# One planned order for attention, router and experts: whole groups of value products, direct router logits, two weight parts staged early

## The chip, the cores and the metric

The kernel runs on one NeuronCore of a Trainium2 chip. The metric is the device time in microseconds (us). The engines are named as the profile names them: PE (TensorE matmul), PEld (its weight loads), DVE (VectorE), ACT (ScalarE), POOL (GpSimd) and SP (SyncE, which here only issues DMAs).

## The reference

Three layers on 4 x 576 tokens. Attention has 8 heads of 64, and keeps in each row only the scores within tau of the row's maximum. A mixture of 8 experts follows, in which each token goes to one expert (512 to 1024 to 512, with relu); a router weighs it. A dense layer ends it (512 to 2048 to 512, leaky relu). All is float32.

```
scores = scale * np.matmul(q, k.transpose(0, 1, 3, 2))
thresh = np.max(scores, axis=-1, keepdims=True) - tau
scores = np.where(scores >= thresh, scores, -1000000000.0)
...
logits = x @ w_gate;  e_idx = np.argmax(logits, axis=1)
eom = 1.0 / (1.0 + np.exp(-(x @ w_output_gate)))
h = np.maximum(x[mask] @ w1[e], 0.0);  ye = h @ w2[e]
out[mask] = gate_w[mask, None] * eom[mask, e, None] * ye
...
h = x @ w_in;  g = np.maximum(0.01 * h, h);  g @ w_out
```

## The kernel before

Work is not issued in program order. Each step (a handful of instructions) is added to a `Plan` with an engine or a choice of two, a cost in us, what it depends on, a priority and the buffers it takes and frees. `Plan.run` places the steps one after another: on each engine it looks when each ready step could start, keeps those within TOL = 0.0499 us of the earliest, and takes among them the one of lowest priority number. The order so found is fixed at build time; on the chip every engine runs its own instructions in that order and waits on semaphores. A step that is late on the chip thus holds up all that stands behind it on its engine. There are two plans: one for attention (with the router and the first expert products at its end) and one for all that follows.

**Attention** handles two heads at a time: 16 pairs, each with 9 tiles of 128 queries. For a tile PE makes the scores (label S, L447, products in float32r, 4 instructions of 288 columns), DVE takes the row maximum (L456), ACT the exponential (L467), DVE masks and sums (L475), PE transposes the result (TR, L504, 4 transposes in float32), and ACT or DVE copies it out of PSUM. The products with the values (AV, L583) need all tiles of a half pair: each half has four chunks of 4 instructions on 64 columns of the array (two heads side by side), and a last chunk on all columns (L589). The plan places the chunks one by one, so that other PE work can come between two of them. Eight PSUM banks are shared: a score tile holds two of them, every transpose and every half of AV one.

**Router logits** per pair: G0 (L641) multiplies with the gate matrix as the stationary operand, 32 columns of the array for each of four token groups; ACT copies the result out (L232, tile g); X1 transposes it back (L654), adds one direct product for the fifth token group (L655, the tokens as the stationary operand, 32 columns streamed) and transposes the fifth group (L656). After the last pair of a batch a chain of small DVE steps ranks tokens.

**First tokens.** `prefix`, at the end of the attention plan, picks the expert with most tokens after three batches, loads the four parts of its first-layer weights into `raw`, and runs the first layer for 216 of its tokens (L1439) on PE while the last batch is being ranked.

**Experts** (second plan). Weights come as 512 KB parts (L1571) through 4 `raw` buffers; each part is cast (hi, L1538) and its remainder taken (lo, L1543), and three products (hi hi, hi lo, lo hi) stand for one in float32. The first tokens' second layer comes first (L1683, parts 4 to 7), then eight windows of tokens, one for each expert, of 400 down to 216 tokens (L1642 first layer, L1683 second). Tokens are gathered by POOL, transposed by PE and cast by ACT and DVE. A branch on a flag (L1991, all engines) stands where the plan reaches t_over = 2.2. Besides, `narrow` (L1289 to L1326) turns the dense layer's weights, whose 8-byte elements are read as pairs of integers, into float32: two staging buffers `dw`, four DVE steps and one ACT step (L1317) for each of 32 blocks. It starts at plan time w_n0 = 30. The dense layer (L1845, L1871) ends the kernel.

Of the kernel before, what the change touches and what calls it, by code (L numbers as in the profile page):

```python
# [61 lines left out]
class Plan:  # L62
# [8 lines left out]
    START, DONE = 1.1, 0.9  # L71

    def __init__(self):
        self.ops = []
        self.dma = 0.0
        self.hook = None
# [16 lines left out]
    def run(self):  # L93
# [11 lines left out]
        for o in self.ops:  # L105
            if o.left == 0:
                enter(o)
        done = []
        while len(done) < len(self.ops):
# [29 lines left out]
            o.eng, o.t0, o.t1 = e, s, s + o.engs[e]  # L139
            engs[e] = o.t1  # L140
            if o.dma:
# [49 lines left out]
def attention(ctx, tc, q, k, v, st):  # L191
# [61 lines left out]
    for P in range(NP):  # L253
# [49 lines left out]
        def turn(o, P=P):  # L303
            T["sw", P] = t = one.tile([128, 9, 2, D], F32R, name="sw")
            nc.scalar.copy(out=t[:, :, 1, :], in_=T["srk", P][:, :, 0, :].bitcast(F32))
            nc.vector.tensor_copy(out=t[:, :, 0, :], in_=T["srk", P][:, :, 1, :].bitcast(F32))
# [49 lines left out]
        for h in range(2):  # L356
            a = pl.add(
                "pe", 0.22, lambda o, P=P, h=h: trs(o, T["srk", P], range(4 * h, 4 * h + 4)), [O["lrk", P], O.get(("k1", P))],
                base + st.w_k[h], acq=[(bk, 1), (r_tp, 1)] + ([(r_k1, 1)] if h == 0 else []), label="trk",
# [8 lines left out]
        a = pl.add(  # L368
            "pe", 0.11, tail_tr, [O["lrk", P], O["lrq", P], O["k1", P]], base + st.w_k[2], acq=[(bk, 1), (r_tp, 1)], label="trt",
        )  # L370
# [9 lines left out]
        for h in range(2):  # L380
            a = pl.add(
                "pe", 0.22, lambda o, P=P, h=h: trs(o, T["srq", P], range(4 * h, 4 * h + 4)), [O["lrq", P], O.get(("qt", P)), *used],
                base + st.w_k[3 + h], acq=[(bk, 1), (r_tp, 1)] + ([(r_qt, 1)] if h == 0 else []),
# [18 lines left out]
        else:  # L402
# [18 lines left out]
            for h in range(3):  # L421
                a = pl.add("pe", 0.22, lambda o, h=h, f=trs2: f(o, h), [sw], -8.2 + h, acq=[(bk, 1), (r_tp, 1)], label="trk2")
# [7 lines left out]
        for i in range(9):  # L430
# [41 lines left out]
            def mask(o, P=P, n=n, h=h, t=t, rP=rP):  # L472
# [11 lines left out]
            s = O["s", n] = pl.add(  # L484
                "pe", 0.98 if i == 8 else 0.49, scores, [O["k2", P], *kev, *qev, O.get(("s", n - 1))], n + st.w_s,
                acq=[(bk, 2), (r_sc, 1)],
# [89 lines left out]
        for half in range(2):  # L576
# [18 lines left out]
            for c in range(5):  # L595
                box = {}
                prev = pl.add(
                    "pe", 0.53 if c < 4 else 0.49,
                    lambda o, f=av, c=c, fb=first: f(o, fb or o, c), [*ready[half], prev, O.get(("av", P))],
                    base + st.w_av + (5 * half + c) * st.d_av, acq=[(bk, 1), (r_av, 1)] if c == 0 else [],  # L600
                    rel=[(r_et, O["t", base]), (r_rv, O["rv", P])] if (half, c) == (1, 4) else [], label="AV",
                )
# [35 lines left out]

        def g0(o, xP=xP, hp=hp):
            for t in range(4):  # L640
                nc.tensor.matmul(  # L641
                    out=bank(o)[32 * t:32 * t + 32, 0:128], lhsT=gd[:, hp, :], rhs=xP[:, t * 128:(t + 1) * 128],
                    start=True, stop=True, tile_position=(0, 32 * t),
                )

        def g0_ev(o, a, P=P):
            T["g", P] = sm_p.tile([128, 128], F32, tag="g", name="g", bufs=2)
            copy(o, T["g", P], bank(a)[:, 0:128])

        ag = O["xo1", P] = pl.add("pe", 0.29, g0, [*xr, gates], wx + 0.1, acq=[(bk, 1), (r_tp, 1)], label="G0")  # L650
        eg = pl.add(AD, evac(128), lambda o, a=ag, f=g0_ev: f(o, a), [ag], wx + 0.5, rel=[(bk, ag), (r_tp, ag)], label="eG0")

        def x1(o, P=P, xP=xP, hp=hp):
# [22 lines left out]

        a1 = O["xo2", P] = pl.add("pe", 0.43, x1, [*xr, eg], wx + 1, acq=[(bk, 1), (r_tp, 1)], label="X1")
        e2 = pl.add("dve", 0.24, lambda o, a=a1, f=x2_ev: f(o, a), [a1, rc], wx + 1.5, label="eX2")
# [712 lines left out]

def prefix(pl, tc, st, R, w1, xrows, done):

# [119 lines left out]
def experts(pl, ctx, tc, st, R, ar, w1, w2, w_in, w_out, xrows, yT, wtab, wf, out):  # L1513
# [44 lines left out]
    for r, n, tw in wins:  # L1558
# [7 lines left out]
        for q in range(4 if r is None else 0, 8):  # L1566
# [9 lines left out]
            def lo(o, ld, h):  # L1576
                t = ar.w(h.slots[r_w][0])
                subtract(o, t[:, 1, :], raw[ld.slots[r_raw][0]], t[:, 0, :].bitcast(F32))

            ld = O["ld", r, q] = prev_ld = pl.add(  # L1580
                "sp", 0.4, load, [rl], need - 24, after=[prev_ld], acq=[(r_raw, 1)], dma=1.6 if r is not None else 0.0,
                lat=0.0 if r is not None else (0.0, 0.0, 2.0, 4.0)[q - 4], label="ld")
            a = O["hi", r, q] = prev_hi = pl.add(
                AD, (1.05, 0.8), lambda o, f=hi, ld=ld: f(o, ld), [ld, prev_hi], need - 12, acq=[(r_w, 1)], label="hi", at=0.0 if r is None else free)
            O["lo", r, q] = pl.add(
                *((("dve", "pool"), (1.5, 2.7)) if r is not None else ("dve", 1.4)), lambda o, f=lo, ld=ld, h=a: f(o, ld, h), [a], need - 11.9, rel=[(r_raw, ld)], label="lo", at=free)
# [325 lines left out]
def tile_attn_moe_mlp(ctx, tc, q, k, v, tau, w_gate, w_ogate, w1, w2, w_in, w_out, out):  # L1912
# [8 lines left out]
    st.nsc, st.ntp, st.nav = 4, 4, 2  # L1921
    st.w_k = [-9.01, -41.3, -10.8, -7.75, -2.8]
    st.w_s, st.w_m, st.w_th, st.w_x, st.w_kk, st.w_t, st.w_te = -0.83, -9.42, -28.19, 3.88, -7.61, 2.26, -14.75
    st.w_l = [-0.74, 7.52]
    st.w_av, st.d_av = 17.36, -0.34
    st.w_xo = 17.33
    st.w_rt, st.w_ch = 11.17, 12.27
    st.w_n0, st.w_n1 = 30, 30
    st.t_over = 2.2
# [5 lines left out]
    st.raw = [raw_p.tile([128, 1024], F32, name=f"raw{i}") for i in range(4)]  # L1935
    st.sm = [raw_p.tile([128, DM], F32, name=f"sm{i}") for i in range(4)]

    xrows = dram.tile([NT, DM], F32, name="xrows")
# [4 lines left out]
    with ExitStack() as order:  # L1943
# [28 lines left out]
        R.wt = rtt  # L1972
        st.prefix = lambda pl, done: prefix(pl, tc, st, R, w1, xrows, done)
        st.batch_done, st.count, st.consts = R.batch, R.count, R.consts
# [6 lines left out]
        with ExitStack() as c2:  # L1981
            p = c2.enter_context(tc.tile_pool(name="ex", bufs=1))
            ar = Arena(p)
            st.ys = [p.tile([128, CAPS[0]], F32, name=f"ys{i}") for i in range(2)]
            st.dw = [p.tile([128, 512, 2], I32, name=f"dw{i}") for i in range(2)]
            st.cv = [p.tile([128, 512], I32, name=f"cv{i}") for i in range(2)]
# [52 lines left out]
```

## Time and profile before

| | us |
|---|---|
| median of 3 runs (1016.75, 1020.75, 1367.39) | 1020.75 |
| profiled execution | 1020.31 |
| its span, first to last instruction | 1018.5 |
| PE busy | 978.2 (96%) |
| DVE busy | 648.4 (64%) |
| ACT busy | 512.5 (50%) |
| POOL busy | 253.2 (25%) |
| mean granted TensorE clock | 0.983 |

Shares are of the whole span. Attention takes its first third, and DVE and ACT are far busier there than the mean shows. A busy PE is not one at its peak: a matmul record covers its time in the pipeline, and what one costs is read from start to start.

### The profile page before, as it was taken

Reading aid. Unit: us, or ns where it says so; the run is one execution under the profiler, and the core shown is the slowest. Engines: PE = TensorE matmul, PEld = TensorE weight load, DVE = VectorE, ACT = ScalarE, POOL = GpSimd, SP = SyncE. Lnnn points to the kernel's source line nnn. Section 1 sums busy time; section 2 is a strip of 40 time slices with the busy share of each in tenths; the row PEclk is TensorE's granted clock in tenths of the full one; section 3 lists DMA queues with packets and bytes.
Section 4 is the critical chain, followed back from the end, with each engine's and each line's share of the span. In section 5 each row is a group of like instructions: output and inputs, shape, how many; then the busy total and the mean of one; then the engine's idle time right before and its main releaser. Section 6 shows DMA issues by size and latency. Waiting matters only on the chain. (4 is left out here: it accounts for less than half of the span.)

```text
span 1018.5 us, 16995 instructions
## 1 busy us (share of the span) xinstructions
PE 978.2 (96%) x6134; PEld 834.6 (82%) x6134; DVE 648.4 (64%) x1255; ACT 512.5 (50%) x1022; POOL 253.2 (25%) x304
## 2 busy tenths in 40 slices
PE   6999999999999799799899999999999999999994
PEld 6777777777787698799899998888888888888883
DVE  6888998998896677997876657994223222322331
ACT  6787787787785253544555535443222322322321
POOL 3433243234121244353424501331000100100000
PEclk9999999999999899799999999999999999999998
DMA  5432432432213588888886753421100200100000
GB/s 145 128 86 60 141 76 71 120 81 64 84 26 104 182 271 257 288 276 271 282 271 209 231 169 93 121 86 42 42 1 1 83 1 0 57 6 1 11 32 21
DMA packets 63580, 114.33 MB, mean 112 GB/s; under 512 B 15424, under 2 KB 32832, under 8 KB 62976
## 3 DMA queue, kind: packets, MB, share of 16 engines
q1 hardware_dynamic: 56912, 92.02, 28.3%
q0 software_dynamic: 6576, 21.15, 7.5%
q8 instruction: 50, 0.82, 0.3%
q14 instruction: 42, 0.34, 0.1%
HBM read 84.72 MB, written 19.09 MB: 102 GB/s over the span
## 5 line engine op out<-in xcount | busy, mean ns | idle before, releaser
L1845 PE MATMUL ps<-arena 128*128 128x512 f32 (+1 forms) x960 | 207.6, 368 | 0.0
L1871 PE MATMUL ps<-arena 128*128 128x512 f32 x864 | 206.7, 389 | 0.0
L1543 DVE TENSOR_TENSOR arena<-raw,arena 128x512 fp32r<-128x512 f32 (+2 forms) x135 | 133.1, 990 | 112.2 <-PE ps L1871 67.1
L1845 PEld LDWEIGHTS ps<-arena 128*128 128x128 f32 x960 | 168.7, 188 | 30.8
L1538 ACT CAST arena<-raw 128x1024 fp32r<-128x1024 f32 (+2 forms) x155 | 123.2, 806 | 131.9 <-PE ps L1871 57.9
L1871 PEld LDWEIGHTS ps<-arena 128*128 128x128 f32 x864 | 161.4, 188 | 33.0
L1856 DVE TENSOR_TENSOR raw<-ps,raw 128x512 f32<-128x512 f32 (+1 forms) x80 | 50.6, 636 | 135.4 <-ACT raw L1852 135.2
L1683 PE MATMUL ps<-arena 128*128 128x216 f32 (+7 forms) x864 | 129.0, 308 | 2.5 <-DVE arena L1656 1.3
L1642 PE MATMUL ps<-arena 128*128 128x400 f32 (+7 forms) x768 | 116.3, 312 | 11.1 <-ACT arena L1538 6.2
L1683 PEld LDWEIGHTS ps<-arena 128*128 128x128 f32 x864 | 123.0, 194 | 3.4 <-DVE arena L1656 1.6
L1642 PEld LDWEIGHTS ps<-arena 128*128 128x128 f32 x768 | 113.1, 194 | 12.6 <-ACT arena L1538 6.7
L456 DVE TENSOR_REDUCE nm<-ps 128x1 f32<-128x576 f32 x144 | 108.7, 755 | 20.5 <-PE ps L447 17.6
L1852 ACT ACTIVATE raw<-ps 128x512 f32<-128x512 f32 (+1 forms) x80 | 44.1, 555 | 152.4 <-PE ps L1845 152.4
L475 DVE SCALAR_TENSOR_TENSOR em<-ps,th,e 128x576 f32<-128x576 f32 x144 | 115.9, 805 | 1.9 <-ACT e L467 1.4
L467 ACT ACTIVATE e<-ps,nm 128x576 f32<-128x576 f32 x144 | 106.7, 742 | 2.5 <-DVE nm L456 2.5
L447 PE MATMUL ps<-k,qt 128*128 128x288 f32 x512 | 104.6, 329 | 1.3 <-DVE em L475 1.0
L447 PEld LDWEIGHTS ps<-k,qt 128*128 128x128 f32 x512 | 75.8, 194 | 31.6 <-DVE em L475 8.2
L232 ACT COPY eta<-ps 128x512 f32<-128x512 f32 (+1 forms) x157 | 83.5, 544 | 25.2 <-PE ps L504 25.0
L1900 POOL DMA_INDIRECT out_dram<-sm,oidx x18 | 17.7, 982 | 304.3 <-ACT sm L1894 271.4
L504 PE MATMUL ps<-ident,em 128*128 128x128 f32 x576 | 85.4, 276 | 0.8 <-DVE em L475 0.8
L583 PE MATMUL ps<-eta,rv 128*64 128x288 f32 x512 | 83.8, 425 | 0.6 <-ACT k L232 0.5
L504 PEld LDWEIGHTS ps<-ident,em 128*128 128x128 f32 x576 | 68.1, 141 | 4.9 <-ACT e L467 2.6
(226 smaller groups left out, 1041.8 us busy)
## 6 DMA issues: line engine op xcount, KB each, us to landing
raw<-in_moe_w_dram SPq DMA_DIRECT2D x72, 512.0 KB, 5.5
k<-k POOLq DMA_DIRECT2D x30, 304.0 KB, 4.1
dw<-in_moe_w_in_dram SPq DMA_DIRECT2D x16, 512.0 KB, 5.3
dw<-in_moe_w_out_dram SPq DMA_DIRECT2D x16, 512.0 KB, 5.2
rk<-in_k_dram SPq DMA_DIRECT2D x16, 256.0 KB, 2.9
rq<-in_q_dram SPq DMA_DIRECT2D x16, 256.0 KB, 3.0
rv<-in_v_dram SPq DMA_DIRECT2D x16, 256.0 KB, 2.7
xrows<-xt SPq DMA_DIRECT2D x4, 1024.0 KB, 4.8
```

Of the source, the lines that this page charges most:

```text
L447: nc.tensor.matmul(out=s[:, c, :], lhsT=lhs, rhs=T[kk, P][:, off + c * HALF:off + (c + 1) * HALF], start=(m == 0), stop=(m == 2 * len(ops) ...
L456: nc.vector.tensor_reduce(out=T["nm", n], in_=T["sc", n], axis=AX.XY, op=ALU.max, negate=True)
L467: nc.scalar.activation(out=T["e", n].rearrange("p (a c) -> p a c", a=2), in_=T["sc", n], func=AF.Exp, bias=T["nm", n][:, 0:1], scale=1.0,)
L475: nc.vector.scalar_tensor_tensor(out=T["em", P, t][:, h, :].rearrange("p (a c) -> p a c", a=2), in0=T["sc", n], scalar=T["th", n][:, 0:1], ...
L504: nc.tensor.transpose(out=bank(o)[:, c * 128:(c + 1) * 128], in_=T["em", P, t][:, h, 64 * h + c * 128:64 * h + (c + 1) * 128], identity=ident,
L583: nc.tensor.matmul(out=out[64 * h:64 * h + 64], lhsT=T["rv", P][:, 4 * h + c, :], rhs=T["eta", P][:, h, c, lo_:lo_ + HALF], start=(c == 0) ...
L1538: nc.scalar.copy(out=out, in_=in_)
L1543: (nc.vector if o.eng == "dve" else nc.gpsimd).tensor_tensor(out=out, in0=in0, in1=in1, op=ALU.subtract)
L1642: nc.tensor.matmul(out=bank(o)[:, 0:n], lhsT=w[:, wi, 128 * f:128 * f + 128], rhs=xx[:, xi, c, :], start=(c == 0 and i == 0), stop=(c == K ...
L1683: nc.tensor.matmul(out=bank(first, d)[:, 0:n], lhsT=w[:, wi, k0:k0 + 128], rhs=hx[:, xi, :], start=(f == 0 and i == 0), stop=(f == 7 and i ...
L1845: nc.tensor.matmul(out=bank(o)[:, 0:n], lhsT=w[:, wi, c, 128 * c2:128 * c2 + 128], rhs=y[:, c, 0:n], start=(k == 0), stop=(k == 3 * KD - 1),)
L1871: nc.tensor.matmul(out=bank(first, t), lhsT=g[:, gi, 128 * t:128 * t + 128], rhs=w[:, wi, c2, :], start=(f == 0 and k == 0), stop=(f == FF ...
```

## The change

Five edits, in one kernel. First, `Plan` gets a price for PE's turn from one kind of step to another: 0.095 from or to AV, -0.08 from float32 to float32r. It is added to the start of a candidate, so that a step of another kind counts as 0.095 later than the next chunk of AV, which is more than TOL. Some PE costs are set anew, and so are the priorities of attention (st.w_...). Second, G0, its copy and the transpose back go; X1 makes the logits of all five token groups as direct products. Third, parts 4 and 5 of the first tokens' second layer are loaded in attention by SP, behind the first-layer parts, into the `dw` buffers, which now exist from the start (`sw` shares the buffers of k2 for that). Their cast and remainder get the lowest plan times, ahead of the branch; the casts of parts 6 and 7 are bound to ACT, and lose their stated load latency of 2 and 4. Fourth, `narrow` starts at 60 and not 30, and its due times end 60 before the dense layer and not 30. Fifth, two small table steps of DVE (`others`, `starts`) come 7 and 14 later.

```
+    def turn(self, a, b):
+        if a is None or not self.KIND:
+            return 0.0
+        a, b = self.KIND.get(a.label, "f"), self.KIND.get(b.label, "f")
+        if a == b:
+            return 0.0
+        if "v" in (a, b):
+            return 0.095
+        return -0.08 if b == "r" else 0.0
...
-                    s = max(t, o.est)
+                    s = max(t + (self.turn(ahead, o) if e == "pe" else 0.0), o.est)
...
+    pl.KIND = {"S": "r", "trk": "r", "trt": "r", "trq": "r", "trk2": "r", "AV": "v"}
...
-                "pe", 0.98 if i == 8 else 0.49, scores, [O["k2", P], ...
+                "pe", 1.064 if i == 8 else 0.532, scores, [O["k2", P], ...
...
-                    "pe", 0.53 if c < 4 else 0.49,
+                    "pe", 0.48 if c < 4 else 0.42,
...
-        ag = O["xo1", P] = pl.add("pe", 0.29, g0, [*xr, gates], wx + 0.1, ...
-        eg = pl.add(AD, evac(128), lambda o, a=ag, f=g0_ev: f(o, a), [ag], ...
         def x1(o, P=P, xP=xP, hp=hp):
-            nc.tensor.transpose(out=bank(o)[:, 0:128], in_=T["g", P], identity=ident)
-            nc.tensor.matmul(out=bank(o)[:, 128:160], lhsT=xP[:, 512:640], rhs=gd[:, hp, :], start=True, stop=True)
+            for t in range(5):
+                nc.tensor.matmul(
+                    out=bank(o)[:, 32 * t:32 * t + 32], lhsT=xP[:, 128 * t:128 * t + 128], rhs=gd[:, hp, :], start=True, stop=True)
             nc.tensor.transpose(out=bank(o)[:, 160:288], in_=xP[:, 512:640], identity=ident)
...
+    for q in range(4, 6):
+        def second(o, q=q):
+            nc.sync.dma_start(out=wview(staged(st, q), q), in_=wpart(w1, w2, st.star, q))
+        last = pl.add("sp", 0.4, second, [last], pr + 1, lat=5.0, label="ld")
...
+            if r is None and q < 6:
+                t = staged(st, q)
+                a = prev_hi = O["hi", r, q] = pl.add("act", 0.3, ... -40 + q, acq=[(r_w, 1)], label="hi")
+                O["lo", r, q] = pl.add("dve", 0.7, ... [a], -40 + q, label="lo")
+                continue
...
-                lat=0.0 if r is not None else (0.0, 0.0, 2.0, 4.0)[q - 4], label="ld")
+                lat=0.0, label="ld", at=free if (r, q) == (0, 1) else 0.0)
-                AD, (1.05, 0.8), lambda o, f=hi, ld=ld: f(o, ld), ...
+                *((AD, (1.05, 0.8)) if r is not None else ("act", 0.2)), lambda ...
...
-    others = pl.add("dve", 1.2, R.others, [], -13, at=free, label="tb")
-    starts = pl.add("dve", 1.3, R.starts, [], 5, at=free, label="tb")
+    others = pl.add("dve", 1.2, R.others, [], -13, at=free + 7, label="tb")
+    starts = pl.add("dve", 1.3, R.starts, [], 5, at=free + 14, label="tb")
...
-    st.w_rt, st.w_ch = 11.17, 12.27
-    st.w_n0, st.w_n1 = 30, 30
+    st.w_rt, st.w_ch = 24.07, -0.65
+    st.w_n0, st.w_n1 = 60, 60
```

## Rows read from the trace of the kernel before

**Rows 1.** Busy us by stretch: PE, PEld, DVE, ACT, POOL; clock, DMA share, GB/s.
```profile
63.40:83.20 19.80, 19.80 (x154) 14.94 (x152) 16.46 (x38) 15.42 (x36) 6.49 (x11) 1.00 0.31 77
103.00:122.70 19.70, 19.70 (x153) 14.84 (x152) 18.30 (x45) 15.08 (x35) 6.12 (x11) 1.00 0.49 144
sum 294.90, PE 294.19 PEld 224.40 DVE 258.59 ACT 231.97 POOL 97.20; mean PE 19.61 PEld 14.96 DVE 17.24 ACT 15.46 POOL 6.48
```
**Rows 2.** PE in order of time, attention: start us, us, engine, line, operation, count.
```profile
27.18 1.01 PE L583 MATMUL ps<-eta,rv 128*64 128x288 f32 x4
...
156.90 0.60 PE L504 MATMUL ps<-ident,em 128*128 128x128 f32 x4
157.43 0.71 PE L583 MATMUL ps<-eta,rv 128*64 128x288 f32 x4
158.07 0.79 PE L447 MATMUL ps<-k,qt 128*128 128x288 f32 x4
...
306.53 0.60 PE L504 MATMUL ps<-ident,em 128*128 128x128 f32 x4
306.88 0.78 PE L447 MATMUL ps<-k,qt 128*128 128x288 f32 x4
...
328.63 2.16 PE L583 MATMUL ps<-eta,rv 128*64 128x288 f32 x16
330.72 0.75 PE L589 MATMUL ps<-etl,vt 128*128 128x288 f32 x2
```
**Rows 3.** The two largest groups of DVE in attention, on the page.
```profile
L456 DVE TENSOR_REDUCE nm<-ps 128x1 f32<-128x576 f32 x144 | 108.7, 755 | 20.5 <-PE ps L447 17.6
L475 DVE SCALAR_TENSOR_TENSOR em<-ps,th,e 128x576 f32<-128x576 f32 x144 | 115.9, 805 | 1.9 <-ACT e L467 1.4
```
**Rows 4.** PE in order of time, the router's products of two pairs.
```profile
306.13 0.27 PE L654 MATMUL ps<-ident,g 128*128 128x128 f32 x1
306.25 0.31 PE L655 MATMUL ps<-gd,xu 128*128 128x32 f32 x2
306.39 0.31 PE L656 MATMUL ps<-ident,xu 128*128 128x128 f32 x1
...
322.02 0.60 PE L624 MATMUL ps<-ident,xu 128*128 128x128 f32 x4
...
322.91 0.59 PE L1419 MATMUL ps<-ident,sm 108*128 108x108 f32 x4
```
**Rows 5.** All engines in order of time, between attention and the experts.
```profile
340.11 6.07 PE L1439 MATMUL ps<-sm,raw 128*128 128x216 f32 x32
...
343.78 0.16 DVE L1089 TENSOR_SCALAR flag<-mcap 128x1 int32<-128x1 f32 x1
344.17 1.99 ACT L1538 CAST arena<-raw 128x1024 fp32r<-128x1024 f32 x2 [11.08 <-DVE flag L1089]
...
349.75 0.57 DVE L1076 TENSOR_TENSOR scr<-one,tsa 128x224 f32<-128x224 f32 x1 [5.81 <-DVEq L1992]
...
351.64 0.67 DVE L1656 SCALAR_TENSOR_TENSOR arena<-ps,arena 128x216 fp32r<-128x216 f32 x2 [0.68 <-SPq L1992]
...
353.50 2.47 PE L1683 MATMUL ps<-arena 128*128 128x216 f32 x10 [0.88 <-DVE arena L1543]
```
**Rows 6.** Busy us by stretch, as in the first group, early in the experts.
```profile
350.00:360.00 10.00, 7.59 (x33) 7.07 (x34) 8.52 (x17) 5.79 (x13) 3.99 (x4) 0.50 0.60 202
...
400.00:410.00 10.00, 5.03 (x29) 4.62 (x28) 9.54 (x11) 5.47 (x8) 4.53 (x4) 0.89 0.93 316
410.00:420.00 10.00, 7.33 (x28) 6.94 (x29) 9.07 (x11) 4.81 (x10) 5.89 (x3) 0.60 1.00 383
```
**Rows 7.** ACT and PE in order of time, at PE's waits in the experts.
```profile
406.56 0.67 ACT L1317 ACTIVATE dw<-dw 128x512 f32<-128x512 f32 x1 [4.17 <-DVE cv L1305]
...
410.73 0.68 PE L1642 MATMUL ps<-arena 128*128 128x368 f32 x1 [5.70 <-ACT arena L1538]
...
488.12 8.84 PE L1642 MATMUL ps<-arena 128*128 128x320 f32 x48 [2.56 <-DVE arena L1656]
```

More of the change, by code (lines that the diff above doesn't have):

```diff
@@ L108, in run @@
         done = []
+        ahead = None
         while len(done) < len(self.ops):
@@ L139, in run @@
             o.eng, o.t0, o.t1 = e, s, s + o.engs[e]
+            if e == "pe":
+                ahead = o
             engs[e] = o.t1
@@ L303, in turn @@
         def turn(o, P=P):
-            T["sw", P] = t = one.tile([128, 9, 2, D], F32R, name="sw")
+            T["sw", P] = t = k1_p.tile([128, 1216], F32R, tag="k2", name="sw")[:, 0:1152].rearrange("p (t a d) -> p t a d", t=9, a=2)
             nc.scalar.copy(out=t[:, :, 1, :], in_=T["srk", P][:, :, 0, :].bitcast(F32))
@@ L484, in attention @@
             s = O["s", n] = pl.add(
-                "pe", 0.98 if i == 8 else 0.49, scores, [O["k2", P], *kev, *qev, O.get(("s", n - 1))], n + st.w_s,
+                "pe", 1.064 if i == 8 else 0.532, scores, [O["k2", P], *kev, *qev, O.get(("s", n - 1))], n + st.w_s,
                 acq=[(bk, 2), (r_sc, 1)],
@@ L636, in attention, with x1 @@
         e0 = pl.add("dve", 0.6, lambda o, a=a0, f=x0_ev: f(o, a), [a0, rc, O.get(("fin", b - 1))], wx + 0.5, rel=[(bk, a0), (r_tp, a0)], label="eX0")
-        def g0(o, xP=xP, hp=hp):
-            for t in range(4):
+        def x1(o, P=P, xP=xP, hp=hp):
+            for t in range(5):
                 nc.tensor.matmul(
[L642 to L653, printed above, removed]
-            nc.tensor.transpose(out=bank(o)[:, 0:128], in_=T["g", P], identity=ident)
-            nc.tensor.matmul(out=bank(o)[:, 128:160], lhsT=xP[:, 512:640], rhs=gd[:, hp, :], start=True, stop=True)
+                    out=bank(o)[:, 32 * t:32 * t + 32], lhsT=xP[:, 128 * t:128 * t + 128], rhs=gd[:, hp, :], start=True, stop=True)
             nc.tensor.transpose(out=bank(o)[:, 160:288], in_=xP[:, 512:640], identity=ident)
@@ L1389, with staged, prefix @@
 PASSES = ((0, 0), (0, 1), (1, 0))
-def prefix(pl, tc, st, R, w1, xrows, done):
+def staged(st, q):
+    return st.dw[q - 4].bitcast(F32).rearrange("p f a -> p (f a)")
+def prefix(pl, tc, st, R, w1, w2, xrows, done):
     nc, bk, ps = tc.nc, st.bk, st.ps
@@ L1578, in lo @@
                 subtract(o, t[:, 1, :], raw[ld.slots[r_raw][0]], t[:, 0, :].bitcast(F32))
+            if r is None and q < 6:
+                t = staged(st, q)
+                a = prev_hi = O["hi", r, q] = pl.add(
+                    "act", 0.3, lambda o, t=t: nc.scalar.copy(out=ar.w(o.slots[r_w][0])[:, 0, :], in_=t), [prev_hi], -40 + q, acq=[(r_w, 1)], label="hi")
+                O["lo", r, q] = pl.add(
+                    "dve", 0.7, lambda o, t=t, h=a: subtract(o, ar.w(h.slots[r_w][0])[:, 1, :], t, ar.w(h.slots[r_w][0])[:, 0, :].bitcast(F32)),
+                    [a], -40 + q, label="lo")
+                continue
             ld = O["ld", r, q] = prev_ld = pl.add(
                 "sp", 0.4, load, [rl], need - 24, after=[prev_ld], acq=[(r_raw, 1)], dma=1.6 if r is not None else 0.0,
-                lat=0.0 if r is not None else (0.0, 0.0, 2.0, 4.0)[q - 4], label="ld")
+                lat=0.0, label="ld", at=free if (r, q) == (0, 1) else 0.0)
             a = O["hi", r, q] = prev_hi = pl.add(
-                AD, (1.05, 0.8), lambda o, f=hi, ld=ld: f(o, ld), [ld, prev_hi], need - 12, acq=[(r_w, 1)], label="hi", at=0.0 if r is None else free)
+                *((AD, (1.05, 0.8)) if r is not None else ("act", 0.2)), lambda o, f=hi, ld=ld: f(o, ld), [ld, prev_hi], need - 12, acq=[(r_w, 1)], label="hi",
+                at=0.0 if r is None else free)
             O["lo", r, q] = pl.add(
-                *((("dve", "pool"), (1.5, 2.7)) if r is not None else ("dve", 1.4)), lambda o, f=lo, ld=ld, h=a: f(o, ld, h), [a], need - 11.9, rel=[(r_raw, ld)], label="lo", at=free)
-    others = pl.add("dve", 1.2, R.others, [], -13, at=free, label="tb")
-    starts = pl.add("dve", 1.3, R.starts, [], 5, at=free, label="tb")
+                *((("dve", "pool"), (1.5, 2.7)) if r is not None else ("dve", 1.4)), lambda o, f=lo, ld=ld, h=a: f(o, ld, h), [a], need - 11.9, rel=[(r_raw, ld)], label="lo", at=free + 3 if r is None else free)
+    others = pl.add("dve", 1.2, R.others, [], -13, at=free + 7, label="tb")
+    starts = pl.add("dve", 1.3, R.starts, [], 5, at=free + 14, label="tb")
     pe = None
@@ L1936, in tile_attn_moe_mlp @@
     st.sm = [raw_p.tile([128, DM], F32, name=f"sm{i}") for i in range(4)]
+    st.dw = [raw_p.tile([128, 512, 2], I32, name=f"dw{i}") for i in range(2)]
     xrows = dram.tile([NT, DM], F32, name="xrows")
@@ L1972, in tile_attn_moe_mlp @@
         R.wt = rtt
-        st.prefix = lambda pl, done: prefix(pl, tc, st, R, w1, xrows, done)
+        st.prefix = lambda pl, done: prefix(pl, tc, st, R, w1, w2, xrows, done)
         st.batch_done, st.count, st.consts = R.batch, R.count, R.consts
```

24 lines of the change are left out of this document (12 added, 12 removed).

## The prediction

> **What bounds the kernel now.** I read the busy time by stretch first, then PE in order of time, then the waits at PE's gaps. Over fifteen pairs of heads [rows 1] PE is busy 294.19 of 294.90 us, 19.66 a pair: PE sets attention's pace. DVE stands close behind, and unevenly: 16.46 of 19.80 in an ordinary pair, 18.30 of 19.70 in a pair where a router chain runs on it (two pairs in four look like that), 17.24 in the mean. ACT has 15.46. So work taken from PE here shortens the kernel only until DVE is full.
>
> What PE pays is seen start to start [rows 2]. A transpose group followed by scores takes 306.88 - 306.53 = 0.35. With one chunk of AV between them it is 158.07 - 156.90 = 1.17, so a chunk alone costs 0.82. Four in a row take 330.72 - 328.63 = 2.09, 0.52 each, and entering them costs 0.53 - 0.35 = 0.18 (157.43 against 156.90). Four chunks cost 2.27 together and 3.28 one by one: each separate run that is saved is worth 1.01 / 3 = 0.34. The timeline of PE has 97 runs of L583, from the one at 27.18 to the one at 328.63, for 16 x 8 = 128 chunks.
>
> Past attention PE loses time at three places. It ends the first tokens' first layer at 346.18 (340.11 + 6.07) and runs their second layer steadily from 353.50 [rows 5]; the next stretch is granted clock 0.50, half speed (1.2 GHz), after that idle time [rows 6]. From 400 to 420 it is busy 5.03 + 7.33 = 12.36 us of 20, idle 7.64, and the clock is 0.60 in the second half. At 488.12 it waits 2.56 [rows 7].
>
> **The change, part by part.**
>
> *Whole groups.* A waiting step of another kind counts 0.095 later than the next chunk, more than the tolerance of 0.0499, so a chunk that is ready always goes next: 16 x 2 = 32 runs are left, 65 fewer. That is 65 x 0.34 = 22 us of PE, 1.38 a pair; PE would need 18.3. Does it arrive? An ordinary pair can come to 19.80 - 1.38 = 18.4, with DVE at 16.5. A router pair cannot go under DVE's 18.30; of its present 1.40 of idle time I leave half, which makes 19.0 to 19.2. The mean is 18.8, and 16 x (19.66 - 18.8) = 13.8; the first and the last pair are not full ones, so I take **-13**. The bounds are -22 (all of PE's saving) and -5 (pairs of 19.35, DVE with as much idle time as now). The plan prices DVE's two large steps at 0.67 and 0.73, the trace has 0.755 and 0.805 [rows 3]: the order is made as if DVE had more room than it has, which is why I stay away from -22. New priorities move router steps to later due times; they stay on DVE.
>
> *Direct logits.* G0 goes with its copy and the transpose back. Now, X0 and G0 take 322.91 - 322.02 = 0.89 [rows 4], of which four transposes at 0.12 (306.25 - 306.13) are 0.48: G0 0.41, the transpose back 0.12, the one direct product 0.14 (306.39 - 306.25), together 0.67. Then: five direct products, 5 x 0.14 = 0.70. That is **0**. Bounds: no quicker than G0's 0.41 in all, -0.26 x 16 = -4; each of the ten passes at the 0.12 of a transpose with weights of its own, 1.20, so +0.53 x 16 = +8. I take the middle one, since the row is the very operation. The page "TensorE: Matmul & The Clock Gate" of the Trainium skill, section LDWEIGHTS, speaks against this part: it gives a weight load's time as columns / 1.2, 107 ns for these 128 columns. By it ten loads come to an estimated 1.07 and the part to about +6; the row of 0.14 for two loads and two passes does not agree. The copy saved on ACT lies beside PE. So do the two new loads: SP issues them in attention's last stretch, where nothing on its queue is due but the first-layer parts, and DMA share in attention is 0.31 to 0.49 [rows 1]; uncovered they would delay only a branch of later loads.
>
> *First tokens' second layer.* In the trace the casts of two parts are done at 346.16 (344.17 + 1.99) and their data was no limit [rows 5]. What is late is DVE: it passes the branch only at 349.75, 5.81 after the flag, does a table step, and has the first remainder of the hidden values at 351.64, of the weights just before 353.50. After the change the two weight remainders stand ahead of the branch. The second can start only after its cast, at 346.16; DVE reaches the branch some 2.2 us later (346.16 - 343.94) and leaves it at about 351.9. ACT has two more casts ahead of it, of some 1 us each. The table step is moved behind. So the hidden values' remainder comes at about 352.6, 1 later than now, but nothing more is missing: PE runs steadily from about 352.7 and not 353.5. I take **-1**. Bounds: +3 (two casts and two remainders, all waited for one after another), -4 (PE from 349.5, DVE's present end of the branch).
>
> *`narrow` 30 us later.* The wait of 5.70 at 410.73 ends with ACT's cast of gathered tokens. ACT stood 4.17 until 406.56 at L1317, a step of `narrow`, behind DVE [rows 7]. `narrow` at 60 has not begun then. The 7.64 idle go, and with them the low clock: after 417.96 PE runs at full speed, so some 5.3 of the 7.33 busy us were at half and cost 2.6. That is -10.2. But the same blocks now come 30 us later, beside windows that are shorter, and DMA share is up to 1.00 here [rows 6]. The event of 488.12 shows what they do there: 2.56, or about 5 with a fall of the clock as dear as the 2.6 above. I count one more such event, +4: **-6**. Bounds: -12 (nothing is given back) and +2 (two long waits come back). The two small table steps on DVE cost nothing, as DVE does them in a later gap; if they delayed PE it would be by no more than their price in the plan, 1.2 and 1.3.
>
> *Sum.* -13 + 0 - 1 - 6 = -20 on the profiled execution's 1020.3 (span 1018.5 and 1.8 around it): **1000**. The median of the runs, 1020.75, is 0.4 above that execution.
>
> **The rivals.**
>
> - *DVE takes the bound over* (17%). Pairs of 19.3, gain 6 and not 13: 1007. For it: router pairs have DVE at 93% already. Against it: ordinary pairs leave 3.3 us.
> - *The narrow wait only moves* (13%). Nothing is won after attention but the 1 us: 1006. For it: DMA share 1.00, and DVE over 9 us of 10 in both stretches where PE waited.
> - *All of it arrives* (15%). Router steps spread over ordinary pairs, 18.3 each: -22 - 1 - 10 = 987. For it: DVE's mean of 17.24 is under 18.3.
> - *Weight loads bound the direct products* (4%), ten passes at 0.12: +8, 1008. The rule on the weight load named above would act so; the row of 0.14 is against it.
> - *Slower: whole groups starve DVE* (4%). While a run of 2.09 us lasts PE makes no scores. If DVE runs dry for x in each of a pair's two runs, a pair takes 17.5 + 2x: no gain from x = 1.1, and with the 7 us won elsewhere the kernel is over 2% slower from x = 1.9. Dry for the whole run, a pair takes 21.7: 16 x 2 - 7 = +25, 1045. Against it: four score tiles may wait in PSUM, more DVE work (1.56 each) than a run lasts.
> - *The groups don't come whole* (2%), say since a half's inputs are late on the chip: only 7 are won, 1013.
>
> **How the numbers follow.** The forecast has 45%, with its own range of 993 to 1007, and its number is the prediction, 1000. The range for eight in ten reaches to the cases at 987 and 1013: **986 to 1014**. 2% of 1020.75 is 20.4 us, about what a measurement of this kernel can tell from no change; the line is at 1000.3. Half of the forecast lies below it (23%), nearly all of the case at 987 (15%), and some 7% of the others, as their parts may add up: **faster 0.45, same 0.50, slower 0.05**, the slower part being the starved DVE and one percent for waits not foreseen.
>
> **What would show it.** Right: 32 runs of the value products in attention, or close to it; ordinary pairs near 18.4, router pairs near 19 with DVE full; five direct products in 0.7; DVE past the branch about 2 us later against the flag, and no wait for a weight remainder after the first; no wait of PE in the first window's end. Wrong: pairs all at 19 or above with gaps on PE that DVE ends; a wait of some 8 us between 430 and 530 after which the clock is low; direct products at 1.1 or more.

## The result, and the profile after

| us | before | after |
|---|---|---|
| median of the runs taken together | 1018.82 (4 runs) | 1007.31 (4 runs, 1004.9 to 1007.89) |
| profiled execution, its span | 1020.31, 1018.5 | 1004.9, 1002.7 |
| granted TensorE clock | 0.983 | 0.991 |

The ratio is 0.9892, 95% interval [0.987, 0.9914]: 11.5 us less by the medians, 15.8 by the two profiled spans. A second set of runs of the same two kernels gave 1005.57 against 1020.34 (0.989, [0.9843, 0.9938]). The forecast was 1000. The ratio leaves out one run before, of 1367.39, and the profiled execution before lies 1.5 above the median of its kernel, the one after 2.4 below.

Where the 15.8 us of the spans came from is read from where PE starts its first product of each stage: the first tokens' first layer (L1439 before, L1455 after), the first window of 400 tokens, and the dense layer.

| stage, us | before | after | difference | forecast |
|---|---|---|---|---|
| attention, to the first tokens' first layer | 333.59 | 321.73 | -11.9 | -13 |
| first tokens, to the first window | 34.92 | 34.49 | -0.4 | -1 |
| the eight windows | 242.83 | 239.17 | -3.7 | -6 |
| dense layer to the end | 407.16 | 407.32 | +0.2 | 0 |

So in this pair of profiles each stage went the way forecast, and a little less far. A second profile of the changed kernel has 320.86, 34.22, 241.59 and 407.23 in the same order: a difference of under 1 us in attention, or of 2.4 in the windows, can be chance, and the -3.7 of the windows would be -1.2 there. Inside attention two terms were wrong, and they cancel. First the busy time by stretch over fifteen pairs of heads, answering to [rows 1]; columns: stretch, length, busy us of PE, PEld, DVE, ACT, POOL, clock, DMA share, GB/s.

```profile
23.00:43.20 20.20, 18.38 (x138) 14.85 (x138) 16.29 (x37) 15.39 (x36) 11.98 (x13) 1.00 0.67 172
...
61.40:80.00 18.60, 18.60 (x153) 15.92 (x152) 16.17 (x37) 14.87 (x35) 6.85 (x14) 1.00 0.26 66
...
117.20:137.40 20.20, 19.20 (x158) 15.99 (x156) 19.37 (x56) 15.59 (x37) 7.36 (x15) 1.00 0.39 79
...
193.30:212.80 19.50, 19.32 (x157) 16.05 (x156) 18.88 (x53) 15.77 (x38) 8.00 (x16) 1.00 0.36 75
...
269.10:289.10 20.00, 18.82 (x154) 16.01 (x153) 18.14 (x55) 15.33 (x36) 2.94 (x12) 1.00 0.15 33
...
sum 283.50, PE 278.81 PEld 235.63 DVE 252.16 ACT 226.23 POOL 96.79; mean PE 18.59 PEld 15.71 DVE 16.81 ACT 15.08 POOL 6.45
```

A pair now takes 283.5 / 15 = 18.90. PE's busy time fell from 294.19 to 278.81, by 15.4; its idle time rose from 0.71 to 4.69, by 4.0. The idle time sits in a few pairs: 1.82 of it in the first, 2.4 in the three in which a router chain runs on DVE (20.2, 19.5 and 20.0 here), while the ordinary pair has PE full at 18.6.

Then PE in order of time, answering to [rows 2, 4]; columns: start, us, engine, line, operation, count.

```profile
107.59 0.72 PE L607 MATMUL ps<-etl,vt 128*128 128x288 f32 x2
108.15 1.20 PE L659 MATMUL ps<-gd,xu 128*128 128x32 f32 x10
109.18 0.31 PE L661 MATMUL ps<-ident,xu 128*128 128x128 f32 x1
...
112.75 2.16 PE L601 MATMUL ps<-eta,rv 128*64 128x288 f32 x16
114.84 0.75 PE L607 MATMUL ps<-etl,vt 128*128 128x288 f32 x2
```

All 128 chunks stand in 32 runs of four, as x16 here (97 runs before). The five direct products take 109.18 - 108.15 = 1.03, not the 0.70 of the forecast. What set the two prices is seen on PEld, first before and then after:

```profile
306.14 0.30 PEld L655 LDWEIGHTS ps<-gd,xu 128*128 128x128 f32 x2
...
107.91 1.33 PEld L659 LDWEIGHTS ps<-gd,xu 128*128 128x128 f32 x10
```

Before, the first of the two weight loads began at 306.14, 0.11 ahead of its pass (306.25), while PE was still at the transpose: a row that counts from the first pass leaves it out. After, ten loads follow one another.

The waits of PE in attention are now (the three largest; columns: who waited for what, us in total, times, longest):

```profile
PE ps L601 <- ACT eta L250: 1.9, 2, 1.2
PE ps L522 <- DVE em L493: 1.3, 2, 1.1
PE ps L465 <- DVE em L493: 0.8, 2, 0.4
```

The first is for ACT's copies of transposes and not for DVE, and its two waits lie in two of the router pairs (0.7 in the one from 117.2, 1.2 in the one from 269.1).

The largest DVE groups on the page answer to [rows 3]; the durations are the same, and the idle time before the two together went from 22.4 to 26.2.

```profile
L493 DVE SCALAR_TENSOR_TENSOR em<-ps,th,e 128x576 f32<-128x576 f32 x144 | 115.6, 811 | 9.2 <-ACT e L485 8.4
...
L474 DVE TENSOR_REDUCE nm<-ps 128x1 f32<-128x576 f32 x144 | 107.3, 752 | 17.0 <-PE ps L465 15.2
```

Between attention and the experts, all engines in order of time [rows 5]:

```profile
331.91 0.15 DVE L1094 TENSOR_SCALAR flag<-mcap 128x1 int32<-128x1 f32 x1
332.30 1.99 ACT L1599 CAST arena<-dw 128x1024 fp32r<-128x1024 f32 x2 [11.59 <-DVE flag L1094]
...
333.38 2.36 DVE L1559 TENSOR_TENSOR arena<-dw,arena 128x1024 fp32r<-128x1024 f32 x2 [1.31 <-ACT arena L1599]
334.20 1.99 ACT L1554 CAST arena<-raw 128x1024 fp32r<-128x1024 f32 x2
338.65 1.81 ACT L1675 ACTIVATE arena<-ps 128x216 fp32r<-128x216 f32 x7 [2.47 <-DVEq L2017]
339.05 3.35 PE L1708 MATMUL ps<-arena 128*128 128x216 f32 x12 [4.74 <-ACT arena L1675]
```

The first layer ends at 334.31, and PE runs the second one without another wait from 339.05, 4.74 later; before it was 7.32 (346.18 to 353.50). That is 2.6 us where 0.8 was forecast, but the stage as a whole gained 0.4. For before, PE was not idle in all of the 7.32: it did 1.69 us of the stage's work in it, which now comes behind 339.05.

```profile
349.30 0.60 PE L1611 MATMUL ps<-ident,sm 108*128 108x108 f32 x4 [3.12 <-DMA sm<-xrows,gidx]
350.18 0.55 PE L1683 MATMUL ps<-arena 128*128 128x216 f32 x1 [0.28 <-ACT arena L1650]
352.08 0.55 PE L1683 MATMUL ps<-arena 128*128 128x216 f32 x1 [1.35 <-DVE arena L1656]
```

So the idle time behind the first layer fell by 0.9, from 5.63 to 4.74, and a wait of 1.44 at the first window takes it back. PE's waits from there on answer to [rows 6, 7]:

```profile
356.21 0.45 PE L1667 MATMUL ps<-arena 128*128 128x400 f32 x1 [1.44 <-ACT arena L1554]
357.96 19.14 PE L1667 MATMUL ps<-arena 128*128 128x400 f32 x95 [1.29 <-DVE arena L1559]
431.34 0.41 PE L1667 MATMUL ps<-arena 128*128 128x324 f32 x1 [1.73 <-ACT arena L1554]
432.22 14.26 PE L1667 MATMUL ps<-arena 128*128 128x324 f32 x95 [0.46 <-DVE arena L1559]
492.42 3.40 PE L1667 MATMUL ps<-arena 128*128 128x296 f32 x23 [1.17 <-DVE arena L1559]
499.81 6.87 PE L1667 MATMUL ps<-arena 128*128 128x296 f32 x48 [1.75 <-DVE arena L1681]
528.44 7.84 PE L1667 MATMUL ps<-arena 128*128 128x272 f32 x60 [0.81 <-DVE arena L1681]
```

The long wait of 5.70 is gone, and no wait in the windows is above 1.75; the last stretch of half clock (1.2 GHz) before the end of the kernel is now at 359.2, 3.4 us long (the second profile has one more, as long, at 501.1, and a longest wait of 2.1). Over the windows PE was idle for 242.8 - 231.7 = 11.1 us before and for 239.2 - 230.4 = 8.8 after, and its busy time fell by 1.3. In the second profile it was idle for 9.5.

### The profile page after: what moved, and what is told of

The parts are those of the page before. It is cut to its first block, busy times and chain, and to the rows that moved or that the text cites. A ratio compares the mean times of both kernels' runs of the same rounds, so it can differ in the third digit from the quotient of the medians.

```text
span 1002.7 us, 16909 instructions
## 1 busy us (share of the span) xinstructions
PE 960.8 (96%) x6118; PEld 844.5 (84%) x6118; DVE 641.3 (64%) x1231; ACT 507.3 (51%) x1009; POOL 264.4 (26%) x325
## 5 line engine op out<-in xcount | busy, mean ns | idle before, releaser
L1559 DVE TENSOR_TENSOR arena<-raw,arena 128x512 fp32r<-128x512 f32 (+2 forms) x131 | 122.7, 941 | 111.1 <-PE ps L1896 67.0
L1667 PE MATMUL ps<-arena 128*128 128x400 f32 (+7 forms) x768 | 114.1, 308 | 8.7 <-ACT arena L1554 3.2
L465 PE MATMUL ps<-k,qt 128*128 128x288 f32 x512 | 99.5, 322 | 2.3 <-ACT qt L256 0.9
L250 ACT COPY eta<-ps 128x512 f32<-128x512 f32 (+1 forms) x152 | 79.4, 543 | 23.3 <-PE ps L522 19.9
L1559 POOL TENSOR_TENSOR arena<-raw,arena 128x1024 fp32r<-128x1024 f32 x23 | 58.8, 2562 | 61.7 <-ACT arena L1554 59.9
L601 PE MATMUL ps<-eta,rv 128*64 128x288 f32 x512 | 69.5, 412 | 1.9 <-ACT eta L250 1.9
```

What stands on the lines that cost most here:

```text
L250: nc.scalar.copy(out=out, in_=in_)
L465: nc.tensor.matmul(out=s[:, c, :], lhsT=lhs, rhs=T[kk, P][:, off + c * HALF:off + (c + 1) * HALF], start=(m == 0), stop=(m == 2 * len(ops) ...
L1559: (nc.vector if o.eng == "dve" else nc.gpsimd).tensor_tensor(out=out, in0=in0, in1=in1, op=ALU.subtract)
L1667: nc.tensor.matmul(out=bank(o)[:, 0:n], lhsT=w[:, wi, 128 * f:128 * f + 128], rhs=xx[:, xi, c, :], start=(c == 0 and i == 0), stop=(c == K ...
```

## The experiments

Four questions: what the direct products cost, what whole groups bring and why not all of it, what the two edits behind attention are worth, and whether another order is better. Medians stand beside the median of the kernel before on the same chip: 1017.54 for the kernels with narrow-array logits, with whole groups alone, without the turn price and with the late `narrow` alone; 1017.83 for those with products twice, with old priorities, with `narrow` at 30 and without staged parts; 1020.34 for the last four.

### What do five direct products cost?

**Twice the direct products, everything else and the order the same.** The second set writes the same values over the first.

```
-            for t in range(5):
+            for t in (*range(5), *range(5)):
```

> The changed kernel with its five direct logit products issued twice in a row (the second five overwrite the first), in the same order of steps on every engine: what one set of five costs the whole. The trace of the changed kernel has 1.05 us a pair from the first of the five to the transpose behind them. Theory A (PE sets the pace, the weight loads are paid in full): 16 x 1.1 = +17 us, about 1024. Theory B (DVE sets the pace, PE has room): under +6, at most 1013.

1020.65, ratio 1.0028 [1.0007, 1.0049]. Attention is 339.07 instead of 321.73, 17.3 longer: 1.08 for each of sixteen pairs. PE in order of time:

```profile
91.45 2.32 PE L659 MATMUL ps<-gd,xu 128*128 128x32 f32 x20
93.60 0.31 PE L661 MATMUL ps<-ident,xu 128*128 128x128 f32 x1
```

Ten products take 93.60 - 91.45 = 2.15, five took 1.03: each product more costs 0.224. One of 0.14 and four of 0.224 are the 1.03 of the changed kernel. So [rows 4] held the price of the first of a series, and every following one costs 0.08 more. All of it is on the path: a pair with idle time on PE became longer by as much as an ordinary one (20.27 to 21.41, 18.61 to 19.72, from its product with `qz` to the next pair's). That also says that DVE's rate is not what makes PE wait in them, or the waits would have shrunk; they are as before:

```profile
PE ps L601 <- ACT eta L250: 1.9, 2, 1.2
PE ps L522 <- DVE em L493: 1.3, 2, 1.1
PE ps L465 <- DVE em L493: 0.7, 2, 0.4
```

By the medians the run is 13.3 above the changed kernel, less than the 17.3 of the traces. Against the old 0.67 the direct products cost 1.03 - 0.67 = 0.36 a pair, or 0.41 by the 1.08 of this run: 6 us over sixteen pairs, as far as PE's own time goes.

**The changed kernel with the old logits on a narrow array** (G0, its copy, the transpose back; planned anew with the same priorities).

```
-            for t in range(5):
-                nc.tensor.matmul(out=bank(o)[:, 32 * t:32 * t + 32], ...
...
+        ag = O["xo1", P] = pl.add("pe", 0.29, g0, ...
+        eg = pl.add(AD, evac(128), ...
...
```

> The changed kernel with the old way of the router's logits (narrow products, copy out, transposed back), all else as changed; the plan orders attention anew. Theory A (PE sets the pace, and the ten weight loads of the five direct products cost 0.35 us more a pair than foreseen, 16 x 0.38 = 6 us): 1007.3 falls to about 1002. Theory B (DVE sets the pace now, so PE's cost is covered): 1007 give or take 1.5. The trace should show the narrow products at 0.41 a pair and the rest of attention's groups unchanged.

1015.27, ratio 0.998 [0.996, 1.0]: neither theory. Attention is 331.65, ten longer, although PE has less to do. The pairs, 18.6 wide before, now scatter between 15.6 and 22.1, and PE waits everywhere:

```profile
PE ps L465 <- DVE em L493: 5.8, 10, 1.9
PE ps L522 <- DVE em L493: 2.8, 4, 1.1
PE ps L522 <- ACT eta L250: 1.4, 3, 0.8
```

Two steps more per pair gave the plan another order, and that order costs more than the products. An edit that is planned anew is not a test of its price.

### What do whole groups bring, and what takes part of it back?

**Before, with whole groups alone** (old priorities and logits; the mask of the second head of a tile is put behind that of the first).

```
...
+    pl.KIND = {"S": "f", "AV": "v"}
...
-                "dve", 0.73 if i < 8 else 0.83, mask, [x, th, O.get(("xo1", P - 3))], ...
+                "dve", 0.73 if i < 8 else 0.83, mask, [x, th, O.get(("xo1", P - 3)), O["em", P, t] if h else None], ...
```

> The kernel before with the whole groups alone: the turn price of 0.095 for AV, none for float32r, old costs, old priorities, old router, old second plan (one more dependency keeps the masks of two heads in order). Theory A: -22 us of PE, of which some 7 are lost to DVE in router pairs: about 1004. Theory B: DVE's plan prices are too low for this, and pairs stay at 19 or more: 1010 to 1014. Rival of both: without the new priorities the groups come at bad times, and it is no faster than 1018.8.

1027.84, ratio 1.0113 [1.0075, 1.0151]: slower. 29 runs of value products, as wanted; PE's busy time over fifteen pairs fell (294.19 to 286.87), but they take 304.40: 17.5 us idle. One pair takes 25.6. The fall of 7.3 is a third of the 23 that 68 runs fewer at 0.34 would give; a PE record covers its time in the pipeline, and in an order with so many waits busy time alone does not give the price of a run.

```profile
117.00:142.60 25.60, 23.68 (x187) 19.63 (x188) 22.71 (x54) 19.65 (x47) 11.54 (x20) 1.00 0.29 72
...
sum 304.40, PE 286.87 PEld 230.27 DVE 265.61 ACT 223.45 POOL 100.72; mean PE 19.12 PEld 15.35 DVE 17.71 ACT 14.90 POOL 6.71
```

```profile
PE ps L464 <- DVE em L492: 8.2, 15, 1.3
PE ps L557 <- DVE em L492: 1.3, 4, 0.6
...
DVE nm L473 <- PE ps L464: 22.2, 30, 4.1
```

The last line is the other side of it: DVE stands 22.2 us without scores, up to 4.1 at a time (15.5 and up to 1.1 in the kernel before, 12.8 and up to 0.9 in the changed one), and PE then waits for the masks of DVE.

**The changed kernel with the old priorities of attention** (and the same link between masks).

```
-    st.w_k = [-17.57, -56.75, -17.26, -9.64, -5.15]
...
+    st.w_rt, st.w_ch = 11.17, 12.27
```

> The changed kernel with attention's priorities (w_k to w_ch) of the kernel before; turn price, costs, direct logits, staging and narrow as changed (one more dependency keeps the masks of two heads in order). Theory A (the whole groups pay only in an order whose priorities fit them; with the old ones PE and DVE wait for each other): attention loses 10 us or more, about 1020 to 1028. Theory B (the priorities do little; the grouping and the costs make the gain): 1005 to 1010.

1022.3, ratio 1.0053 [1.0034, 1.0072]: 31 runs of value products, attention 340.19, slower than before.

**The changed kernel without the price of a turn to or from AV** (and the same link between masks).

```
-    pl.KIND = {"S": "r", "trk": "r", "trt": "r", "trq": "r", "trk2": "r", "AV": "v"}
+    pl.KIND = {"S": "r", "trk": "r", "trt": "r", "trq": "r", "trk2": "r"}
```

> The changed kernel with the turn price from and to AV taken out, so that other PE work may come between two chunks again (one more dependency keeps the masks of two heads in order). Theory A: some 60 more runs of AV at 0.34 us are 20 us of PE; some 5 us of DVE's waits in router pairs vanish in exchange: about 1021. Theory B (DVE sets the pace): not over 1012, with DVE near 17.5 of each pair either way.

1038.56, ratio 1.0196 [1.0164, 1.0228]: 86 runs, attention 358.32. Most of the runs are single again (62 of 86), as in the kernel before; the time went far past it. So these groups and these priorities are worth something only together: either alone is slower than the kernel before. Priorities searched for single chunks, or for the groups alone, were not run, nor was the link between masks by itself.

**Another order for the same work.** The changed kernel without the staged parts, with other priorities for attention, another tolerance and another surcharge on DVE (PEN) where a step may go to ACT or DVE.

```
+    pl.PEN, pl.TOL = 0.2329, 0.0312
...
-    st.w_av, st.d_av = 17.36, -0.31
+    st.w_av, st.d_av = 19.23, -0.78
...
-    st.w_rt, st.w_ch = 24.07, -0.65
+    st.w_rt, st.w_ch = 35.59, 0.22
```

> The changed kernel without the staged parts (measured at 1003.5), with the same steps in attention and only other priorities, another tolerance and another price for DVE in the attention plan. Theory A (what attention still loses, some 5 us of PE's waits, is a matter of order): pairs at 18.5 in the router pairs too, attention 2 to 5 us shorter, 999 to 1002. Theory B (DVE bounds the router pairs, so no order helps): attention at 321 to 323, 1003 to 1005, the same waits at other places. A worse order than the present one would show as over 1006.

1003.51, ratio 0.9886 [0.9836, 0.9936]. Attention ends 3.2 earlier (318.51) than in the run without staged parts and the old order (321.67), although its first score came 1.4 later (11.67 against 10.25). Fifteen pairs:

```profile
116.50:135.90 19.40, 19.27 (x158) 16.09 (x157) 18.77 (x53) 15.81 (x38) 7.90 (x16) 1.00 0.36 69
...
229.90:248.30 18.40, 18.40 (x152) 15.72 (x151) 15.71 (x35) 15.60 (x36) 6.84 (x13) 1.00 0.21 52
...
sum 280.30, PE 278.46 PEld 235.11 DVE 251.78 ACT 231.12 POOL 96.26; mean PE 18.56 PEld 15.67 DVE 16.79 ACT 15.41 POOL 6.42
```

PE has the same work (278.46 against 278.81) and 1.84 us idle against 4.69. So 2.9 of the 4.0 us of new idle time were order. In the three router pairs PE's idle time went from 2.4 to 0.2; what is left lies in the first pair (0.98) and in two others. The router pairs are still longer than the ordinary ones, 19.4 against 18.4, but PE's records fill them (19.27 of 19.40), while DVE is busy for 18.8: PE does not wait for DVE there. Six short products of the ranking are part of the 0.9; the rest is not accounted for. The whole kernel is not measurably faster: the windows took 240.96 here and 238.00 in the other run, within what two profiles of one kernel differ by.

**The same with the old logits** and priorities of their own.

> As c_dir, with the old narrow-array logits (G0, copy, transpose back) in place of the direct products, and priorities of its own. From start to start G0 cost 0.67 a pair and the direct products 1.05, 6 us over sixteen pairs. Theory A (the price of the direct products is all on the path, and the 1015 of the first run with G0 was its order): attention at 314 to 319, 996 to 1001. Theory B (G0's second leg through ACT costs PE more in waits than the 0.38 a pair that it saves): 1004 or more, with waits of X1 for the copy.

1011.98, ratio 0.9913 [0.9882, 0.9944]. Its trace is of an execution of 1021.6, so it serves for the order alone. G0 and its second leg should take less of PE, but the ordinary pair is no shorter: PE has small gaps in each.

```profile
82.90:101.50 18.60, 18.48 (x155) 15.25 (x153) 16.19 (x37) 15.45 (x35) 6.70 (x12) 1.00 0.33 83
```

Whether an order exists in which the old logits keep their 6 us stays open; the two that were run don't. So the 6 us are what the direct products take of PE beyond the old steps; that the exchange as a whole lost them is not shown.

### What are the edits behind attention worth?

Staged parts and the late `narrow`, each alone and neither. The kernel before with `narrow` at 60 and 60:

```
-    st.w_n0, st.w_n1 = 30, 30
+    st.w_n0, st.w_n1 = 60, 60
```

> The kernel before with narrow at 60 and its due times ending 60 before the dense layer; nothing else. Theory A (its steps ahead of ACT's casts made the long wait near 410): the wait of 5.7 and the low clock behind it go, shorter waits come back later: -4 to -6, about 1014. Rival (the wait only moves by 30 us): 1018 to 1020, with one wait of over 5 us between 430 and 530.

1014.49, ratio 0.9959 [0.9943, 0.9974]. The changed kernel with 30 and 30:

> The changed kernel with narrow at 30 and 30 again. Theory A (narrow's start decides the wait of PE at the end of the first full window): a wait of 5 us or more comes back there, with a low clock behind it: 1010 to 1014. Rival (staging and the later table steps had removed that wait already): 1006 to 1008, no wait of over 2 us there.

1005.64, ratio 0.9893 [0.9859, 0.9928]. The changed kernel without the staged parts, with the table steps at their old times:

```
-    for q in range(4, 6):
-        def second(o, q=q):
...
-    others = pl.add("dve", 1.2, R.others, [], -13, at=free + 7, label="tb")
...
+    others = pl.add("dve", 1.2, R.others, [], -13, at=free, label="tb")
...
```

> The changed kernel without the staging: parts 4 and 5 of the first tokens' second layer come through raw after attention as before, with their remainders behind the branch and the two table steps at their old times; attention and narrow as changed. Theory A (staging moves DVE's branch later by as much as it saves behind it): 1006 to 1009, and the stretch from the first layer to the first window within 1 us of 34.5. Rival (it spares a wait for weights): 3 us slower or more, 1010 or above.

1003.54, ratio 0.9866 [0.9839, 0.9893]. And with neither:

> The changed kernel's attention with neither of the edits behind it: no staged parts, narrow at 30 and 30, the table steps at their old times. Theory A (either narrow late or the staged parts take away the wait near 410 of the kernel before; with neither it comes back, 5 us and a stretch at half clock): 1007 to 1009, a PE wait above 4 us near 398. Theory B (that wait hung on how attention ended, not on these edits): 1003 to 1005 and no such wait.

1007.28, ratio 0.9877 [0.9847, 0.9907]. With the old attention the late `narrow` is worth 0.4% by the ratio. With the new attention the times don't tell the four versions apart: neither edit has 0.9877, both 0.9892 and 0.989, so the whole measured gain is there without them. What the edits do is read from the stages, each from one profile, with the chance differences given above:

| us | first tokens to first window | eight windows | longest wait of PE in the windows |
|---|---|---|---|
| neither, old attention (before) | 34.92 | 242.83 | 5.70 |
| neither, new attention | 35.18 | 244.59 | 5.34 |
| late `narrow`, old attention | 34.35 | 238.66 | 2.37 |
| late `narrow`, new attention | 34.03 | 238.00 | 2.39 |
| staged parts, new attention | 34.18 | 239.88 | 2.34 |
| both (changed kernel, two profiles) | 34.49, 34.22 | 239.17, 241.58 | 1.75, 2.1 |

With neither edit the long wait is back, and half clock with it (10.2 us from 396.5):

```profile
399.08 0.67 PE L1653 MATMUL ps<-arena 128*128 128x368 f32 x1 [5.34 <-ACT arena L1549]
401.69 12.50 PE L1653 MATMUL ps<-arena 128*128 128x368 f32 x59 [1.94 <-DVE arena L1554]
```

Either edit alone takes it away; both together are no better than one. Behind other orders of attention long waits stand in spite of both edits: 3.88 in the first window and 5.23 at 550.62 with the narrow-array logits, 3.86 in the first window with the old priorities (profiles of executions 11.0 and 4.9 above the medians of those two). With `narrow` late and nothing staged it is:

```profile
394.05 0.44 PE L1653 MATMUL ps<-arena 128*128 128x368 f32 x1 [1.83 <-ACT arena L1549]
395.36 16.31 PE L1653 MATMUL ps<-arena 128*128 128x368 f32 x95 [0.87 <-DVE arena L1554]
431.63 15.57 PE L1653 MATMUL ps<-arena 128*128 128x324 f32 x95 [2.39 <-DVE arena L1554]
```

This version has no wait at the first window, where the changed kernel waits 1.44 and 1.29, as do the others with staged parts.

**The changed kernel once more**, beside the last runs:

> The changed kernel as it is, for the comparison on one chip with the three others: 1007 (1005 to 1009).

1005.57, ratio 0.989 [0.9843, 0.9938]. No version that was run is measurably faster than it: the two lowest medians, 1003.51 and 1003.54, have ratios whose intervals overlap its own.

## Why the prediction came out as it did, point by point

- **Whole groups** (-13 forecast). The 32 runs came, and PE's saving of 22 fits: 15.4 of busy time fell over fifteen pairs, with some 6 of direct products taken in, so about 21 were saved. That it is the groups' alone is argued, since costs and priorities changed with them. The step that failed is "A router pair cannot go under DVE's 18.30", with "I leave half" of the idle time there: 9 us were written off, and only 4.0 were lost, 1.8 of them in the first pair. Five pairs of fifteen were above 19, 2.9 of the 4.0 us were a matter of order, as the other priorities showed, and in that order PE fills the router pairs. The term was about -18, as the rest of the -11.9 when the +6 below is taken out.
- **The plan's prices for DVE** were my reason to stay away from -22: 0.67 and 0.73 against 755 and 805 ns. That reading was wrong. A DVE instruction begins before the one ahead of it is over:

```profile
88.96 0.75 DVE L474 TENSOR_REDUCE nm<-ps 128x1 f32<-128x576 f32 x1
89.63 0.81 DVE L493 SCALAR_TENSOR_TENSOR em<-ps,th,e 128x576 f32<-128x576 f32 x1
```

  From start to start the row maximum takes 0.67, the price of the plan. PE was read from start to start; DVE's two steps should have been too. The busy time by stretch is free of this: it counts once what two records share.
- **Direct logits** (0 forecast, bounds -4 and +8). This is the step that failed: "5 x 0.14 = 0.70", taken since "the row is the very operation". The row had one product, whose first weight load lay beneath the transpose ahead of it, and its price is not that of the next ones; the five take 1.03, just under the 1.1 that the prediction named as a sign of being wrong, and the part cost 6 us of PE. The page "TensorE: Matmul & The Clock Gate" of the Trainium skill, section LDWEIGHTS, was cited against it with 107 ns for a weight load, by estimate about +6 for the part. The runs agree with that: 0.224 for the two passes of a product is 112 ns a pass. A transpose streams 128 columns and not 32, and takes as long (0.12 in [rows 4]): the columns streamed don't set the price. The rival "weight loads bound the direct products" had 4%, and it was the case.
- **First tokens' second layer** (-1 forecast). The way was right (remainders ahead of the branch, PE steady earlier). The working had a slip, as the second remainder's own 1.22 us is not in its 2.2, and the branch was not the fixed 5.81 that it took: DVE ended the remainders 3.7 us behind the flag (335.74 against 332.06), and ACT and DVE still had their first steps behind the branch within 7.2 us of the flag (338.65, 339.27), where DVE's remainder came 7.7 behind it before. PE was steady 2.6 sooner, but 1.69 of that is work that it had done while it waited, and the rest came back as a wait that the prediction didn't name: the first window's tokens are cast by ACT and their remainder taken by DVE later, and PE waits 1.44 and 1.29 for them. Without the staged parts the stage takes 34.03 and with them 34.49 or 34.22: the edit is worth nothing that was measured.
- **`narrow` later** (-6 forecast). The wait of 5.70 went, as said, and part of it was given back, as said, but as five waits of 0.46 to 1.75 after the first window and no single long one. Idle time fell by 2.3 and busy time by 1.3: -3.7 and not -6, and -1.2 in the second profile. The rival by which the wait only moves was wrong: alone, the late `narrow` made the kernel before faster by 0.4% (1014.49 against 1017.54). That the wait goes with either of the two edits was not foreseen.
- **Rivals.** "DVE takes the bound over" is not borne out in any pair: with 1.1 us more in each pair PE's waits did not shrink, and in another order they were nearly gone where DVE has most to do. "Slower: whole groups starve DVE" was the wrong mechanism for this kernel and the right one for its parts: with whole groups and the old priorities DVE stands 22.2 us without scores, PE waits for its masks, 17.5 us idle, and the kernel is slower.
- **The sum.** By terms -18 + 6 - 0.4 - 3.7 = -16.1, against 15.8 of the spans. The forecast of -20 is off by the direct products, for the larger part; the too small term of the groups made up for most of it, which is luck: two errors of 5 and 6 us of opposite sign in one stage. The medians show 4 us less than the profiled pair, since the profiled execution after was the fastest of its four and the one before lay above its median; their 11.5 is about what attention alone gives.

## What to carry to other kernels

A price taken from one short series of instructions holds for its first member; before a longer series is costed by it, look for a row in which the same operation follows itself, and where there is none, take the dear bound. In a kernel whose order is planned ahead, an edit that changes one price or one step changes the order of everything: a saving on the bounding engine arrives only with priorities that fit it, and the same instructions in another order ranged here from 37 us slower in attention (358.32) to 3 us faster (318.51). Two edits that remove the same wait don't add up.

## What the runs showed of the hardware

- Passes with 32 columns streamed and other weights each time cost 112 ns each within a series; the first two of a series cost 0.14 together, as the first weights are loaded beneath the work ahead (306.14, for a pass at 306.25).
- Two large DVE instructions in a row overlap by some 80 ns (0.75 long, the next one 0.67 behind its start), so the durations of DVE's instructions, added up, overstate what it needs: 0.75 and 0.81 are 1.56 for the two, where the plan's 0.67 and 0.73 are 1.40.
- At the branch ACT is idle for 2.47 us, from the end of its last cast (336.19) to its next step (338.65), although it had four casts ahead of it; in the trace of before, with two casts ahead, it was 3.62 (346.16 to 349.78).
